# Sparse attention and a two-layer MLP in one kernel: local q and k as rows of nine tokens, and a new order for the first two batches

## The chip, the cores and the metric

One core of one Trainium2 chip runs the whole program. The time is device microseconds of one execution; the median of several runs is compared. TensorE (PE) does matmuls and transposes, VectorE (DVE) and ScalarE (ACT) elementwise work and everything that reads PSUM, GpSimd (POOL) elementwise work between SBUF tiles and the loads that cast, SyncE (SP) plain loads, stores and transposing DMAs.

## What is computed

```python
scores = q @ k.T / sqrt(64)            # 8 batches, 8 heads, 576 tokens, 64 elements
# heads 0..3 (local):   token i sees j with 0 <= i - j < 32
# heads 4..7 (strided): token i sees j <= i with j % 32 == i % 32
attn = softmax(where(mask, scores, -1e9))
x = (attn @ v) as 4608 rows of 512     # row = batch and token
h = x @ w_in                           # 512 x 2048
g = max(h, 0) + alpha * min(h, 0)      # alpha has 2048 entries
out = g @ w_out                        # 2048 x 512, float32
```

The kernel works in float16 with float32 sums.

## The kernel before

**Pairs and pieces.** Each batch has four pairs of heads: 0 and 1 local, 2 and 3 strided; pair number g = 4 * batch + pair. The work on a pair is cut into pieces:

- `Sc(g, i)` or `score_both(g)`: scores of half a pair or of all of it, the mask, and the exponential on ACT (L397 to L421 for batch 0, where the mask is added by a matmul of the constants; L455 to L487 later, where it is multiplied in on DVE or POOL).
- `Pv(g, i)`: attention times v with a column of ones (L508), the reciprocal (L515) and the scaling (L517) on DVE.
- `X(g)`: PE transposes the result (L531) and ACT or DVE copies it into `xT`, the ring of transposed rows for layer 1.
- `T(u, nm)`: PE transposes of the local q or k of a batch (L295), copied out by ACT and DVE (L235, L237).
- `F(nm, pr)`: the strided q or k of batch 0, loaded as float32 on 72 partitions (L149, eight tokens of a head to a partition) and transposed by PE as they are (L162). `G(nm, pr)`: the same for batch 1 from float16 (L174). From batch 2 on a transposing DMA does it (`transpose_d`, L184).

**Local q and k.** A load (L112 on POOL or SP, L879 for batch 0 on SP) brings eight tokens to a partition, 64 partitions to a head, so 512 tokens of 576. The last 64 tokens, the tail, come by loads of their own (`load_tail`, L209, two issues on POOL for a batch). POOL casts to float16 (`cast_l`, L239), `T` transposes eight blocks, and two more transposes (L325) and two copies serve the tails.

**v.** `load_v` fetches strided v (L219, then copied into `vs` beside the ones) and local v in overlapping blocks of 128 rows (L227); `over_v` copies the overlap of 32 rows for batches 0 and 1.

**Layers.** Rows are treated in chunks of 512. Layer 1 (`lin1_piece(n, m)`, L684) makes 16 pieces of a chunk, each four matmuls of 128x512 into one PSUM bank; ACT takes the negative part (L692) and DVE makes `gT` from it (L695). Layer 2 follows: `U` and `W` for chunk 0 (L970, L985), `lin2_piece` for chunk 1 (L723), and a form with sums and fewer products from chunk 2 on (L809).

**PSUM.** Eight banks: the pool `ps` has three (transposes, Pv), `ph` has three (layer banks, some scores, the dummy matmuls' `wps`), and `sp` takes two. A pool's tiles are given out in turn.

**Order.** Every engine runs its instructions in the order in which the program writes them (`keep`). The start is a list written by hand: nine dummy matmuls `warm(9)` (L851), then

```python
F("q", 0), F("k", 0), F("q", 1), Sc(2, 0), F("k", 1), Sc(2, 1), vs(0), w(1), Sc(3, 0), w(1), Pv(2, 0),
Sc(3, 1), Pv(2, 1), T(0, "q"), w(1), Pv(2, 2), w(1), T(0, "k"), X(2), alpha, Pv(3, 0), Sc(0, 0), w(1),
Pv(3, 1), Sc(0, 1), Pv(3, 2), w(1), Sc(1, 0), w(1), X(3), Sc(1, 1), Pv(0, 0), w(1), Pv(0, 1), L(0),
Pv(1, 0), L(1), X(0), Pv(1, 1), L(2), X(1)
```

`w(n)` are n dummies, `vs(0)` copies strided v on DVE, and `L(m)` begins piece m of layer 1 with its first two matmuls. Layer 1 of chunk 0 follows, then a second list that weaves `U` and `W` with the attention of batch 1, and from chunk 1 on a loop that takes attention pieces between the matmuls.

**Queues.** SP issues, in this order: first q load, constants 0:128 (the identity, from which DVE makes the float32 `id32`, L893), second q load, the other constants (L868), local q and k of batch 0, `alpha`. ACT issues the two first k loads. POOL issues strided v, tails, local v, w_in part 0, cast of q, w_in 1, cast of k, w_in 2 and 3; it then clears the padding rows of `qsd`, `ksd` and `x16s`, does `over_v(0)`, and issues batch 1's loads and w_out. Batch 2's loads are issued inside the second list's stretch.

Of the kernel before, what the change touches and what calls it, by code (L numbers as in the profile page):

```python
# [9 lines left out]
F32 = mybir.dt.float32  # L10
# [22 lines left out]
def kernel(  # L33
# [23 lines left out]
    tpool = ctx.enter_context(tc.tile_pool(name="tl", bufs=4))  # L57
# [40 lines left out]
    def load_qk(b, strided, nm):  # L98

        h0 = 4 if strided else 0
        src = q if nm == "q" else k
        if strided and b:
            t16 = hpool.tile([128, 2, 512], F16, tag=f"{nm}s", bufs=2, name=f"{nm}s")
            cast16[(b, True, nm)] = t16
        else:
            t16 = hpool.tile([128, 2, 512], F32, tag=f"{nm}l", bufs=2, name=f"{nm}l")
            loaded[(b, strided, nm)] = t16
        base = src[b, h0 : h0 + 1, 0:1, :]  # L110
        eng = nc.sync if (b > 2 and not strided) or (b == 0 and strided) else nc.gpsimd
        keep(eng.dma_start(t16, bass.AP(  # L112
            tensor=base.tensor, offset=base.offset,
            ap=[[8 * D, 64], [2 * S * D, 2], [S * D, 2], [1, 8 * D]])))
# [3 lines left out]
    def load_rows(b, nm):  # L118

        src = q if nm == "q" else k  # L120
        t16 = hpool.tile([128, 2048], F16, tag=f"{nm}l", bufs=2, name=f"{nm}r")
# [23 lines left out]
    def first_load(nm, pr, eng):  # L145

        src = q if nm == "q" else k
        t32 = gsum[2 * pr + (nm == "k")].rearrange("p a c -> p (a c)").bitcast(F32)[0:72]
        keep(eng.dma_start(  # L149
            t32.rearrange("p (h e) -> p h e", h=2),  # L150
            src[0, 4 + 2 * pr : 6 + 2 * pr, :, :].rearrange("h (p t) d -> p h (t d)", t=8)))
        loaded[(nm, pr)] = t32

    def turn_first(nm, pr):
# [3 lines left out]
        for h in range(2):  # L158
            pool, tag = (phpool, "hps") if h else (pspool, "ps")
            tp = pool.tile([128, 512], F32, tag=tag, name="tf")  # L160
# [25 lines left out]
    def cast_s(b, nm, eng):  # L186
        t16 = hpool.tile([128, 2, 512], F16, tag=f"{nm}s", bufs=2, name=f"{nm}s")
        if eng[0] == eng[1]:
            cast_copy(eng[0], t16, loaded[(b, True, nm)])
        else:  # L190
            for f in range(2):
                cast_copy(eng[f], t16[:, f : f + 1, :], loaded[(b, True, nm)][:, f : f + 1, :])
        cast16[(b, True, nm)] = t16

    def cast_l(b, nm, eng="pool"):
        t16 = hpool.tile([128, 8, 2, 64], F16, tag=f"{nm}l16", bufs=2, name=f"{nm}l16")
        cast_copy(eng, t16, loaded[(b, False, nm)].rearrange("p f (t d) -> p t f d", t=8))
        cast16[(b, False, nm)] = t16

    def load_tail(b, strided):  # L200

        t16 = tpool.tile([128, 512], F16, tag="tl", name="tl16")
        for i, src in enumerate((q, k)):
            if strided:
                keep(nc.gpsimd.dma_start(
                    t16[32 * i : 32 * i + 32, :].rearrange("x (h c) -> x h c", h=4),
                    src[b, 4:8, 512:576, :].rearrange("h (x c) d -> x h (c d)", c=2)))
            else:
                keep(nc.gpsimd.dma_start(  # L209
                    t16[64 * i : 64 * i + 64, 0:256].rearrange("p (h d) -> p h d", h=4),  # L210
                    src[b, 0:4, 512:576, :].rearrange("h p d -> p h d")))
        cast16[(b, strided, "tail")] = t16

    def load_v(b, strided):


        if strided:
            st = spool.tile([128, 2048], F16, tag="v", bufs=2, name="stv")
            keep(nc.gpsimd.dma_start(  # L219
                st[0:72, :].rearrange("p (h e) -> p h e", h=4),  # L220
                v[b, 4:8, :, :].rearrange("h (p t) d -> p h (t d)", t=8)))
            loaded[b] = st
        else:
# [3 lines left out]
            keep(nc.gpsimd.dma_start(  # L227
                v16[r0:128, :, 0:64],
                bass.AP(tensor=base.tensor, offset=base.offset - (32 - r0) * D,
                        ap=[[D, 128 - r0], [96 * D, 24], [1, D]])))  # L230
# [18 lines left out]
    def over_v(b, eng):  # L249

        v16 = vls[b % 2]
        cast_copy(eng, v16[0:32, 1:24, :], v16[96:128, 0:23, :])
# [28 lines left out]
    def transpose_piece(u, nm):  # L281
# [5 lines left out]
        b, strided = u // 2, u % 2 == 1  # L287
        early = b < NEARLY
        src = cast16[(b, strided, nm)]
        dst = qTs[u % 2][:, :, 0:576] if nm == "q" else kTs[u % 2][:, :, 32:608]  # L290
        tp = pspool.tile([128, 8, 64, 2], F16, tag="ps", name="tp")
        for j in range(8):
            blk = (src[:, j % 2, 128 * (j // 2) : 128 * (j // 2) + 128] if strided
                   else src[:, j].rearrange("p f d -> p (f d)"))
            keep(nc.tensor.transpose(tp[:, j].rearrange("r p e -> r (p e)"), blk, ident))  # L295
        if strided:
            main = tp.rearrange("r j p e -> r e j p")
            o = dst.rearrange("r e (j p) -> r e j p", j=8)[:, :, :, 0:64]
        else:
            main = tp.rearrange("r t p e -> r e p t")  # L300
            o = dst[:, :, 0:512].rearrange("r e (p t) -> r e p t", t=8)
        if early:
            for e in range(2):
# [3 lines left out]
                if nm == "k" and e == 1:  # L307
                    tails(b, u, strided)
# [3 lines left out]
        if nm == "k":  # L312
            tails(b, u, strided)

    def tails(b, u, strided):
# [258 lines left out]
    def X(g):  # L574
        return lambda: x_piece(pairs[g])
# [503 lines left out]
```

## Time and profile before

| | |
|---|---|
| median of 3 runs | 311.73 us (311.38 to 311.92) |
| the profiled execution | 311.1 us, span 309.2 us |
| mean granted clock of TensorE | 0.983 |
| PE busy | 295.7 us, 96% of the span |
| DVE, POOL, ACT busy | 217.0, 185.4, 174.7 us |

The profile is one execution. A line of a group names its source line, engine, operation, what it writes and reads, count, busy time, mean duration and the idle time before it with what ended most of it. A line of the timeline begins with the start in microseconds and the duration; in brackets stands the engine's idle time before it and what ended that. A busy PE is not PE at its peak: at half the granted clock the same matmuls stay busy for twice as long.

### The profile page before, as it was taken

The page shows a single profiled execution, that of the slowest core. Times are in us where ns is not written, and L with a number is a line of the kernel's source. Part 1 is how long each engine was busy: PE and PEld are TensorE (multiplying, and loading weights), DVE is VectorE, ACT ScalarE, POOL GpSimd, SP SyncE. Part 2 cuts the span into 40 slices and gives each one's busy share as a digit, 9 for nine tenths or more (in the row PEclk, how much of TensorE's full clock was granted, in tenths as well). Part 3 has the DMA queues.
Part 4 walks back from the last instruction along what each step waited for, and adds up shares of the span by engine and source line. Part 5 has one row for each costly group of instructions (what it writes and reads, how often), then busy time and mean ns, then how long its engine had stood idle before and what let it go on. Part 6 is the DMA issues. An engine that isn't in the chain of part 4 may idle for free.

```text
span 309.2 us, 6819 instructions
## 1 busy us (share of the span) xinstructions
PE 295.7 (96%) x2676; PEld 183.9 (59%) x2676; DVE 217.0 (70%) x406; ACT 174.7 (57%) x328; POOL 185.4 (60%) x175
## 2 busy tenths in 40 slices
PE   6798999799999999999999999999999999999995
PEld 2464445444455447854785478447845874685484
DVE  2356878647877589668966896689579948935861
ACT  2355672549645775577547755775476446525630
POOL 6398327633977999879897989394835403101300
PEclk9579999999999999999999999999999999999999
DMA  7999995999879597999999999997920040012003
GB/s 176 241 191 184 202 226 149 168 150 278 218 76 184 123 126 91 110 212 131 157 125 201 102 160 143 219 117 87 208 55 5 19 147 10 2 55 83 0 2 137
DMA packets 99584, 40.72 MB, mean 132 GB/s; under 512 B 78160, under 2 KB 95904, under 8 KB 99552
## 3 DMA queue, kind: packets, MB, share of 16 engines
q0 software_dynamic: 53696, 17.84, 60.4%
q1 hardware_dynamic: 45544, 21.86, 34.4%
q10 hardware_dynamic: 312, 0.59, 0.7%
q8 instruction: 21, 0.34, 0.5%
q14 instruction: 11, 0.09, 0.1%
HBM read 38.11 MB, written 9.44 MB: 154 GB/s over the span
## 4 chain that ended last, share of the span: by engine, by line
PE 76%; DVE 10%; ACT 6%; issue 3%; DMA 3%; POOL 1%; SPq 0%; ACTq 0%; DVEq 0%
PE hps L684 31%; PE ops L809 24%; PE ops L723 5%; DVE gT L695 4%; PE pv L508 4%; PE ops L970 3%; ACT neg L692 3%; DMA gsum<-in_q_dram 3%; DVE x L517 2%; PE sp L455 2%; DVE gsum L753 1%; PE xp L531 1%; PE sph L455 1%; PE tp L295 1%; ACT et L484 1%
## 5 line engine op out<-in xcount | busy, mean ns | idle before, releaser
L684 PE MATMUL hps<-xT,win 128*128 128x512 f16 x576 | 131.9, 379 | 1.1 <-DVE gT L695 0.6
L695 DVE SCALAR_TENSOR_TENSOR gT<-neg,oma,hps 128x512 f16<-128x512 f32 x144 | 105.8, 744 | 37.8 <-ACT neg L692 28.9
L692 ACT ACTIVATE neg<-hps 128x512 f32<-128x512 f32 x144 | 85.9, 597 | 37.5 <-PE hps L684 35.3
L684 PEld LDWEIGHTS <-win 128*128 128x128 f16 x576 | 53.8, 98 | 60.7 <-issue 1.9
L480 POOL TENSOR_TENSOR et<-et,consts 128x576 f16<-128x576 f16 (+1 forms) x24 | 34.7, 1445 | 37.0 <-ACT et L478 36.9
L753 POOL TENSOR_TENSOR gsum<-gT 128x1024 f16<-128x1024 f16 x14 | 29.7, 2122 | 42.2 <-DVE gT L695 37.2
L809 PEld LDWEIGHTS <-gsum 128*128 128x128 f16 x448 | 40.9, 98 | 7.1 <-DVE gsum L753 1.8
L809 PE MATMUL ops<-wsum,gsum 128*128 128x256 f16 x328 | 41.5, 273 | 0.2
L809 PEld LDWEIGHTS <-gT 128*128 128x128 f16 x336 | 31.5, 98 | 5.4 <-issue 0.3
L517 DVE TENSOR_TENSOR x<-pv,rc 96x384 f16<-96x384 f32 (+2 forms) x62 | 33.0, 532 | 2.1
L508 PEld LDWEIGHTS <-et 72*128 72x128 f16 (+1 forms) x448 | 24.3, 99 | 13.8 <-issue 2.2
L487 POOL TENSOR_TENSOR et<-et,consts 128x576 f16<-128x576 f16 (+1 forms) x24 | 31.4, 1309 | 0.0
L809 PE MATMUL ops<-wout,gT 128*128 128x256 f16 x224 | 27.9, 273 | 0.1
L478 ACT ACTIVATE et<-sp 128x576 f16<-128x576 f32 (+1 forms) x24 | 15.5, 644 | 17.2 <-PE sp L455 17.2
L515 DVE RECIPROCAL rc<-pv 72x6 f32<-72x6 f32 (+2 forms) x80 | 14.7, 184 | 13.3 <-PE pv L508 13.1
L764 DVE TENSOR_TENSOR osb<-ops,par 128x512 f32<-128x512 f32 (+1 forms) x14 | 9.4, 673 | 16.1 <-PE ops L809 8.2
L484 ACT ACTIVATE et<-sph 128x288 f16<-128x288 f32 (+1 forms) x48 | 18.8, 409 | 0.0
L762 ACT COPY osb<-ops 128x512 f32<-128x512 f32 x14 | 8.2, 585 | 16.8 <-PE ops L809 16.7
L508 PE MATMUL pv<-vs,et 72*128 72x65 f16 x256 | 16.1, 196 | 0.4 <-ACT xT L536 0.3
L723 PE MATMUL ops<-wout,gT 128*128 128x512 f16 x64 | 16.4, 379 | 0.0
L826 ACT COPY par<-ops 128x512 f32<-128x512 f32 x13 | 7.6, 585 | 13.5 <-PE ops L809 13.5
L455 PEld LDWEIGHTS <-kT 64*128 64x128 f16 x392 | 8.4, 95 | 10.5 <-issue 8.0
(109 smaller groups left out, 347.0 us busy)
## 6 DMA issues: line engine op xcount, KB each, us to landing
out_dram<-osb SPq DMA_DIRECT2D x35, 256.0 KB, 2.9
stv<-in_v_dram POOLq DMA_DIRECT2D x8, 288.0 KB, 7.9
vl<-in_v_dram POOLq DMA_DIRECT2D x6, 384.0 KB, 8.7
win<-in_moe_w_in_dram POOLq DMA_DIRECT2D x4, 512.0 KB, 10.2
wout<-in_moe_w_out_dram POOLq DMA_DIRECT2D x4, 512.0 KB, 12.3
qsd<-in_q_dram POOLq DMA_DIRECT2D x7, 288.0 KB, 6.9
ksd<-in_k_dram POOLq DMA_DIRECT2D x7, 288.0 KB, 7.3
ql<-in_q_dram SPq DMA_DIRECT2D x3, 512.0 KB, 7.7
```

What stands on the lines that cost most here:

```text
L455: keep(nc.tensor.matmul(sps[y][:, w * x : w * x + w], P.kT[hf, k0 : k0 + 128], P.qT[hf, q0 : q0 + w], start=(x == 0), stop=(x == len(grp) ...
L480: keep(nc.gpsimd.tensor_tensor(mv, mv, m, op=ALU.mult))
L484: keep(nc.scalar.activation(ev[:, n * y : n * y + n], sps[y][0:r, 0:n], AF.Exp, scale=SCALE))
L487: keep(nc.gpsimd.tensor_tensor(mv, mv, m, op=ALU.mult))
L508: keep(nc.tensor.matmul(pv[:, 65 * x : 65 * x + 65], et[0:r, c : c + 128], v16[0:r, 2 * P.pr + hh, t, :] if P.strided else v16[:, 6 * (2 * ...
L517: keep(nc.vector.tensor_tensor(P.x16[0:w, c0 : c0 + 64 * nb].rearrange("r (c e) -> r c e", e=64), pvv[:, :, 0:64], rc[0:w, 0:nb].unsqueeze ...
L684: keep(nc.tensor.matmul(hps, win16[:, kk, 128 * m : 128 * m + 128], xT[:, kk, c0 : c0 + 512], start=(kk == 2), stop=(kk == 1)))
L692: keep(nc.scalar.activation(neg, hps, AF.Relu, scale=-1.0))
L695: keep(nc.vector.scalar_tensor_tensor(gTs[n][:, m, :], neg, oma[:, m : m + 1], hps, op0=ALU.mult, op1=ALU.add))
L723: keep(nc.tensor.matmul(ops, gTs[n][:, kf, 128 * mt : 128 * mt + 128], wout16[:, kf, :], start=(kf == 0), stop=(kf == 15)))
L753: keep((nc.vector if eng == "dve" else nc.gpsimd).tensor_tensor(gsum[i][:, hs], a, b, op=op))
L809: keep(nc.tensor.matmul(o, lhs(y), rhs(y), start=(first and y == 0), stop=(y == 7), skip_group_check=True))
```

## The change

Local q and k are loaded as nine tokens to a partition, which covers all 576 tokens; the tail loads are gone. `T` transposes eight of the nine blocks as before and `tails` the ninth of q and of k, with outputs at a stride of nine. The first loads take 80 partitions for 72 (the last eight run into the next head's rows and are not used). Strided and local v of batch 0 come in two loads each. The constants are cut at 488 for 128, `alpha` goes ahead of the local loads, the rest of the constants goes last. The dummies are 17 and then 12 for 9 and then 8. The padding rows are cleared by DVE. The lists of batches 0 and 1 have a new order; `over_v` is cut into a POOL half and a DVE half for batch 0 and goes to DVE for batch 1. In chunk 0 the layer-1 pieces 3 to 5, 9 to 11 and 15 take a bank of `ps`, four pieces are begun ahead for three, and three of batch 1's `G` stand between its last pieces. Batch 2's v casts and its DMA transposes go ahead of the loop, as do a strided and a local v load of batch 3 within it.

```diff
-        t16 = hpool.tile([128, 2, 512], F32, tag=f"{nm}l", ...)
+        t32 = hpool.tile([128, 2, 576], F32, tag=f"{nm}l", bufs=2, name=f"{nm}l")
...
-        eng = nc.sync if (b > 2 and not strided) or (b == 0 and strided) else nc.gpsimd
+        eng = nc.gpsimd if b in (1, 2) else nc.sync
...
-            ap=[[8 * D, 64], [2 * S * D, 2], [S * D, 2], [1, 8 * D]])))
+            ap=[[9 * D, 64], [2 * S * D, 2], [S * D, 2], [1, 9 * D]])))
...
+            tensor=base.tensor, offset=base.offset, ap=[[8 * D, 80], [S * D, 2], [1, 8 * D]])))
...
-            pool, tag = (phpool, "hps") if h else (pspool, "ps")
-            tp = pool.tile([128, 512], F32, tag=tag, name="tf")
+            tp = pspool.tile([128, 512], F32, tag="ps", name="tf")
...
+        o = dst.rearrange("r e (p t) -> r e p t", t=9)[:, :, :, 0:8]
...
+    def tails(b, u):
+        tt = pspool.tile([128, 2, 64, 2], F16, tag="ps", name="tt")
+        for i, nm in enumerate("qk"):
+            keep(nc.tensor.transpose(
+                tt[:, i].rearrange("r p e -> r (p e)"),
+                cast16[(b, False, nm)][:, 8].rearrange("p f d -> p (f d)"), ident))
...
-            hps = phpool.tile([128, 512], F32, tag="hps", name="hps")
+            pool, tag = (pspool, "ps") if n == 0 and m // 3 % 2 else (phpool, "hps")
+            hps = pool.tile([128, 512], F32, tag=tag, name="hps")
...
-    keep(nc.sync.dma_start(consts[:, 0:128], consts_dram[:, 0:128]))
+    keep(nc.sync.dma_start(consts[:, 0:488], consts_dram[:, 0:488]))
     first_load("k", 1, nc.scalar)
     first_load("q", 1, nc.sync)
-    keep(nc.sync.dma_start(consts[:, 128:848], consts_dram[:, 128:848]))
...
-    load_l(0, "q")
-    load_l(0, "k")
     keep(nc.sync.dma_start(alpha_r, moe_alpha.rearrange("(kf p) -> kf p", p=128)))
+    load_qk(0, "q")
+    load_qk(0, "k")
+    keep(nc.sync.dma_start(consts[:, 488:848], consts_dram[:, 488:848]))
...
+    for nm in "qk":
+        keep(nc.vector.memset(qks[nm][64:80], 0.0))
+    keep(nc.vector.memset(x16s[64:80], 0.0))
...
     load_v(0, True)
-    load_tail(0, False)
     load_v(0, False)
-    load_w(0, False)
-    cast_l(0, "q")
-    load_w(1, False)
-    cast_l(0, "k")
-    load_w(2, False)
-    load_w(3, False)
+    for c in range(4):
+        load_w(c, False)
...
-    warm(9)
+    warm(17)
     for fn in [
+        F("q", 0), w(1), F("k", 0), w(2), F("k", 1), Sc(2, 0), w(1), Sc(2, 1), alpha, w(1), F("q", 1), w(2),
+        vs(0, 0), vs(0, 1), w(1), Pv(2, 0), Cl(0, "q"), Sc(3, 0), Pv(2, 2), Cl(0, "k"), Pv(2, 1), Sc(3, 1),
+        Pv(3, 0), T(0, "q"), w(1), Pv(3, 2), w(1), X(2), T(0, "k"), w(1), Pv(3, 1), w(1), ov(0, "pool", 0, 12),
+        Sc(0, 0), Sc(0, 1), X(3), Pv(0, 0), ov(0, "dve", 12, 24), Sc(1, 0), Pv(0, 1), Sc(1, 1), Pv(1, 0), L(0),
+        Pv(1, 1), L(3), L(2), X(0, "act"), X(1), L(1)]:
         fn()
+    load_d(1)
+    load_v(1, True)
+    load_w(0, True)
+    load_w(1, True)
+    load_qk(1, "q")
+    load_qk(1, "k")
+    load_w(2, True)
+    load_v(1, False)
+    load_w(3, True)
+    mid = {13: ("q", 0), 14: ("k", 0), 15: ("q", 1)}
     for m in range(16):
         lin1_piece(0, m)
         attn_n(0, 0)
+        if m in mid:
+            G(*mid[m])()
...
-        U(0), sc1(6), U(1), vs(1), U(2), sc1(7), U(3), U(4),
-        Pv(6, 0), U(5), Pv(6, 1), U(6), Pv(6, 2), U(7), Pv(7, 0), U(8), Pv(7, 1), X(6), U(9), Pv(7, 2), U(10),
-        T(2, "q"), U(11), X(7), T(2, "k"), sc1(4), W(0), W(1), sc1(5), W(2), Pv(4, 0), W(3), Pv(4, 1), W(4),
-        Pv(5, 0), X(4), W(5), Pv(5, 1), U(12), X(5), U(13), U(14), U(15), W(6), W(7)]:
+        U(0), Cl(1, "q"), G("k", 1), vs(1, 0), vs(1, 1), sc1(6), U(1), U(2), sc1(7), U(3), U(4), Cl(1, "k"), loads2,
+        Pv(6, 0), Pv(7, 0), Pv(6, 2), U(5), Pv(7, 1), U(6), T(2, "q"), Pv(7, 2), U(7), T(2, "k"), U(8), Pv(6, 1),
+        X(7, "dve"), W(0), W(1), sc1(4), U(9), W(2), sc1(5), W(3), ov(1, "dve", 0, 24), W(4), U(10), X(6), U(11),
+        Pv(4, 1), W(5), Pv(4, 0), U(12), Pv(5, 1), U(13), U(14), Pv(5, 0), U(15), W(6), X(5), X(4), W(7)]:
         fn()
+    for pr in range(2):
+        cast_v(2, pr, "pool")
     wide["on"] = False
-    load_unit(3, False)
+    transpose_d()
+    load_qk(3, "q")
+    load_qk(3, "k")
```

253 lines of the change are left out of this document (67 added, 186 removed).

## The prediction

> **What bounds the kernel now.** I read the page first: busy shares, slices, and the chain that ended last.
>
> ```profile
> PE 295.7 (96%) x2676; PEld 183.9 (59%) x2676; DVE 217.0 (70%) x406; ACT 174.7 (57%) x328; POOL 185.4 (60%) x175
> PEclk9579999999999999999999999999999999999999
> PE 76%; DVE 10%; ACT 6%; issue 3%; DMA 3%; POOL 1%; SPq 0%; ACTq 0%; DVEq 0%
> ```
>
> PE sets the end. The only slices with a low granted clock are the second and third, so I cut the span by stage (columns: PE, PEld, DVE, ACT, POOL busy with counts, clock, DMA share, GB/s).
>
> ```profile
> 0.00:10.00 10.00, 5.42 (x26) 2.45 (x27) 2.36 (x13) 2.08 (x3) 4.76 (x12) 0.94 0.83 197
> 10.00:20.00 10.00, 9.62 (x94) 6.74 (x94) 4.35 (x10) 4.47 (x11) 6.89 (x7) 0.55 1.49 208
> 20.00:31.00 11.00, 9.14 (x119) 5.73 (x119) 6.91 (x20) 6.18 (x13) 10.00 (x15) 1.00 1.21 190
> 44.00:66.60 22.60, 20.55 (x226) 11.02 (x223) 15.10 (x37) 9.29 (x21) 14.80 (x17) 1.00 1.18 144
> 66.60:83.70 17.10, 16.72 (x135) 8.19 (x134) 12.27 (x20) 14.03 (x27) 8.73 (x9) 1.00 1.19 259
> 101.80:133.00 31.20, 31.14 (x315) 20.81 (x314) 24.27 (x45) 20.64 (x38) 29.68 (x28) 1.00 1.03 109
> ```
>
> From 101.8 us on PE has 31.14 busy of 31.20: nothing is to be had there, and the change leaves that work alone. PE idle is 4.6 us before 10, 1.9 in 20 to 31, 2.05 in 44 to 66.6, 0.4 after. The stretch from 10 to 20 looks busy but runs at a clock of 0.55. So the change can move the first 31 us, a little of 44 to 66.6, and hardly anything later. Half-microsecond windows date the clock:
>
> ```profile
> 8.00:8.50 0.50, 0.00 (x0) 0.00 (x0) 0.46 (x1) 0.18 (x1) 0.00 (x0) 1.00 1.12 248
> 9.00:9.50 0.50, 0.00 (x0) 0.00 (x0) 0.00 (x0) 0.00 (x0) 0.00 (x0) 0.50 1.15 281
> 18.50:19.00 0.50, 0.50 (x5) 0.23 (x3) 0.22 (x1) 0.20 (x1) 0.50 (x1) 0.50 1.33 234
> 19.00:19.50 0.50, 0.50 (x9) 0.38 (x8) 0.18 (x1) 0.50 (x2) 0.50 (x2) 1.00 1.19 199
> ```
>
> It fell between 8.5 and 9.0 and came back at 19.0. The timeline of the start says why (start, us, engine, line, out<-in, count, idle before and what ended it):
>
> ```profile
> 1.19 4.02 PE L851 MATMUL wps<-wrm 128*128 128x512 f16 x9 [1.19 <-DVE wrm L887]
> 1.22 0.36 SPq L865 DMA_DIRECT2D consts<-consts  x1
> 1.41 0.90 POOL L219 DMA_DIRECT2D stv<-in_v_dram  x1 [0.25 <-issue]
> 2.06 0.37 SPq L868 DMA_DIRECT2D consts<-consts  x1
> 6.53 0.19 DVE L893 CAST id<-consts 72x72 f32<-72x72 f16 x1 [4.33 <-DMA consts<-consts]
> 6.78 1.22 PE L162 MATMUL tf<-id,gsum 72*128 72x72 f32 x16 [1.56 <-DVE id L893]
> 9.83 1.22 PE L162 MATMUL tf<-id,gsum 72*128 72x72 f32 x8 [1.83 <-DMA gsum<-in_q_dram]
> 12.04 0.65 ACT L421 ACTIVATE et<-sp 72x576 f16<-72x576 f32 x1 [1.03 <-PE sp L413]
> 13.37 1.42 DVE L237 COPY vs<-stv 72x1024 f16<-72x1024 f16 x2
> 25.47 0.19 DVE L515 RECIPROCAL rc<-pv 96x6 f32<-96x6 f32 x1 [1.42 <-PE pv L508]
> 28.72 0.46 DVE L237 COPY xT<-xp 128x576 f16<-128x576 f16 x1 [0.40 <-PE xp L531]
> 29.23 1.24 PE L684 MATMUL hps<-xT,win 128*128 128x512 f16 x5 [0.33 <-DVE xT L237]
> 31.07 11.38 PE L684 MATMUL hps<-xT,win 128*128 128x512 f16 x52 [0.60 <-DVE gT L695]
> ```
>
> Nine dummy matmuls end at 5.21, PE waits until 6.78 for the identity, runs 16 float transposes, and waits 1.83 us for the second q load, which stands ahead of the first scores in PE's order. The next eight transposes take the 1.22 us that sixteen took before: the gate has closed. It opens again only after the solid stretch up to 19.0.
>
> **The change, part by part.** Sums are made against the profiled execution, 311.1 us with a span of 309.2; the median of the runs shown is 311.73, 0.63 above it.
>
> *Dummies and order up to the first exponential.* Seventeen dummies replace nine. One takes 4.02/9 = 0.447 us at the start and 11.38/52 = 0.219 at full clock; the sixteen fast transposes show that the gate was open by 6.78. If it opens at about 5.2 as here, eight more end at 6.95; if it stays closed, 1.19 + 17 x 0.447 = 8.8. The identity now needs the larger constant transfer, 122 KB in place of 32. Its landing is bounded by the two transfers of the trace:
>
> ```profile
> consts<-consts SPq DMA_DIRECT2D x1, 180.0 KB, 8.8
> consts<-consts SPq DMA_DIRECT2D x1, 32.0 KB, 5.3
> stv<-in_v_dram POOLq DMA_DIRECT2D x1, 288.0 KB, 11.1
> kl<-in_k_dram SPq DMA_DIRECT2D x1, 512.0 KB, 11.5
> ```
>
> That is 1.22 + 5.3 = 6.5 or 1.22 + 8.8 = 10.0. I take 6.9, near the small one: both stand behind the first q load alone, while the 180 KB transfer stood behind the second q load too. Then three groups of eight transposes at 1.22/2 = 0.61 and three dummies at 0.22 give 6.95 + 2.5 = 9.45, and scores with their mask some 0.65 (0.99 at half clock, from 11.05 to 12.04): the first exponential starts at about 10.1, against 12.04. The second q load leaves this path; its transposes come after both score groups. The wait of 1.83 goes, and what is late next is v: the strided v lands at 1.41 + 11.1 = 12.5, while the first exponential would be done at 10.8. v now comes in two halves, so one of the two copies (1.42/2 = 0.71 each) lies before that landing, and DVE is free for the first reciprocal at 12.5 + 0.71 = 13.2. That covers late dummies as well: a first exponential at 12.0 costs nothing.
>
> *From there to the first full matmul of layer 1.* Counted on DVE, the engine with the longest chain:
>
> ```profile
> L517 DVE TENSOR_TENSOR x<-pv,rc 96x384 f16<-96x384 f32 (+2 forms) x62 | 33.0, 532 | 2.1
> L515 DVE RECIPROCAL rc<-pv 72x6 f32<-72x6 f32 (+2 forms) x80 | 14.7, 184 | 13.3 <-PE pv L508 13.1
> 20.60 0.69 DVE L237 COPY kT<-tp 128x512 f16<-128x512 f16 x1
> ```
>
> Ten Pv pieces at 0.532 + 0.184 = 7.2, a k copy 0.69, a tail copy some 0.2, the xT copy 0.46, half the overlap copy (moved here from POOL, 12 blocks of 65 columns, estimated at 0.6 from the 0.46 of 576 columns): 9.2, and 1.0 for the small gaps between 25 instructions. With no wait layer 1 could start at 13.2 + 10.2 = 23.4. Waits are added: DVE's idle time in 20 to 31 was 11.00 - 6.91 = 4.1, which gives 27.5 as the other end. I take 1.6, since one round trip from k's transposes through scores and exponential to the first local Pv must stay (1.42 at 25.47): 25.0, against 29.23.
>
> *Banks.* Before, layer 1 had three banks: at 31.07, after a stall of 0.60 for the first gT, 64 - 52 = 12 matmuls were done. Now four pieces are begun ahead (8 matmuls) and pieces 3 to 5, 9 to 11 and 15 use the other pool, so piece 6 is the first to wait for a gT. Twelve are done at 25.0 + 4 x 0.219 = 25.9: the gain up to here is 31.07 - 25.9 = 5.2.
>
> *Queues.* POOL no longer issues ten tail loads and no longer clears the three padding tiles; DVE does that, inside its 4.33 us of waiting for the constants. POOL's casts grow by an eighth (nine tokens for eight), under cover of loads that are in flight anyway. All four w_in loads are issued at once; on the one software queue they still stand behind v, as the first did before. Batch 1's loads are issued earlier, and the tails' small packets are gone, so the later loads stand no further back. The local q and k loads grow from 512 to 576 KB each, and the first loads from 288 to 320: 256 KB more ahead of the k cast, about 1.0 us at the 248 to 281 GB/s of the windows above. k would land by 3.24 + 11.5 + 1.0 = 15.7 and be cast by 15.7 + 1.04 x 9/8 = 16.9, earlier by what the tails' packets took; its transposes, behind q's, I place at about 16.5. That is just about covered, so a later landing is a rival below.
>
> ```profile
> 3.24 0.61 SPq L879 DMA_DIRECT2D kl<-in_k_dram  x1
> 14.81 1.04 POOL L239 CAST kl<-kl 128x1024 f16<-128x1024 f32 x1 [0.24 <-DMA kl<-in_k_dram]
> 43.92 0.81 PE L970 MATMUL ops<-wout,gT 128*128 128x512 f16 x3
> ```
>
> *Chunk 0's layer 2 with batch 1's attention (from 43.92).* Three of the four transposes of batch 1 move into the end of layer 1, and the list is reordered so that consecutive pieces wait less for a bank. Of PE's 2.05 idle I take 0.5 as saved; the ends are all of it, and a loss of 1.0 because the whole overlap copy of batch 1 (by the same estimate 1.2) now stands on DVE ahead of the local Pv pieces. *Batch 2 and 3:* v casts, DMA transposes and a v load leave the first steps of the next loop; of 0.4 idle there I take 0.2.
>
> Sum: 5.2 + 0.5 + 0.2 = 5.9 faster, 311.1 - 5.9 = 305.2 for a profiled execution and 311.73 - 5.9 = 305.8 for the median.
>
> Beside the clock rows: the Trainium skill, "TensorE: Matmul & The Clock Gate", Part 1: The HAM clock gate, says that the gate judges activity in free-running windows of about 3.4 us, and that the ramp costs under 1% of a typical kernel, so one should not fit to a count of cold matmuls. The trace agrees with windows and not with the 1% (an estimate by that page, 3.1 us here): 10 us at half clock can hide up to 5 us of work. By the page's figure the gain to layer 1 would be at most 3.1 + 1.0 for the banks, and the sum 4.8.
>
> **The rivals.** *The gate closes again* (chance 0.14). Between 12.5 and 19 PE waits for DVE again and again, and I count it busy for some 60 to 75% of that time. A stretch with 1.22 us of work in 3.4 closed it above; the 83% of 20 to 31 did not. If it closes once more, up to 3.4 us of work run at half speed before layer 1: about 2.8 lost, gain 3.1, 308.6.
>
> *Loads come late* (0.10). If the larger transfers put the local k 3 us later than 14.7, its cast (about 1.2) ends at 18.9, 2.4 after the transposes could start: layer 1 at 27.4, gain 3.5, 308.2. For it: DMA runs at a share over 1.1 from 5 us on. Against: the tails are gone.
>
> *Slower: the constants hold up everything* (0.09). If the 122 KB land like the 180 KB, at 10.0, PE idles from 6.95 to 10.2, the gate closes as before, and three groups at 1.22 with three dummies at 0.447 bring the scores to 15.2, 4.2 later than before. With the 14.9 us from first exponential to layer 1 of the forecast, stretched to 16 by the closed gate, layer 1 starts at 32.2; less 1.7 for banks and later parts the kernel is 1.3 slower, and 0.2 slower unstretched: 312.5 in the middle. It decides from a landing at about 9.3 on. The Trainium skill, "DMA: Bandwidth & Descriptors", Why a DMA increments its semaphore by 16 and not by 1, says that such a load uses the largest count of engines up to 16 that divides its rows: 12 for 72 rows, 16 for 80; by that the first loads would clear the way sooner and this rival would deserve half its chance. No view shows single engines.
>
> *It does nothing that shows* (0.02): v's landing sets the start however the order is. Against it, v was in at 12.5 and the first reciprocal came only after 13.37 + 1.42 = 14.8.
>
> **How the numbers follow.** The forecast has 0.65, with its own range from 303.2 to 307.6 (layer 1 from 23.4, with 1.0 more out of the later parts, to 26.8). Most likely 305.8. The range of 303.6 to 309.4 takes in the two partial gains and leaves out the slower case, no change and the forecast's best end, together about 0.2. Faster by over 0.2% (0.6 us, about what a measurement of this kernel can tell from no change): 0.65 + 0.14 + 0.10 = 0.89; same 0.02; slower 0.09.
>
> **What would show it.** The clock row should stay at full from the second slice on; first float transposes near 7.0 with no wait between groups; first exponential near 10; first reciprocal near 13.4, waiting for v; layer 1 in full near 25.0 and no wait for gT on PE in chunk 0; U's first matmul near 38. Wrong, if PE idles over a microsecond ahead of the first transposes, if a half clock appears after 10 us, or if layer 1 starts after 28.

## The result and the profile after

| | before | after |
|---|---|---|
| median | 311.70 us (311.38 to 312.04, 6 runs) | 306.68 us (306.46 to 307.54, 6 runs) |
| ratio | | 0.9842, 95% interval 0.9828 to 0.9856 |
| span of the profiled execution | 309.2 us | 304.5 us |
| mean granted clock | 0.983 | 1.000 |

The change gains 5.0 us where 5.9 were forecast; the time lies 0.9 above the number given and inside its range. The page of the changed kernel, in the same three lines as before:

```profile
PE 294.4 (97%) x2688; PEld 182.3 (60%) x2688; DVE 223.4 (73%) x413; ACT 176.1 (58%) x326; POOL 175.6 (58%) x163
PEclk9999999999999999999999999999999999999999
PE 79%; DVE 10%; ACT 6%; issue 2%; DMA 2%; SPq 0%; DVEq 0%; ACTq 0%
```

The clock is full in every slice. The windows (PE, PEld, DVE, ACT and POOL busy with counts, clock, DMA share, GB/s) say the same, and the last one says something new:

```profile
0.00:10.00 10.00, 8.64 (x53) 4.38 (x54) 4.92 (x17) 2.48 (x4) 7.42 (x18) 1.00 0.86 202
10.00:20.00 10.00, 8.16 (x116) 5.09 (x116) 6.90 (x19) 6.13 (x12) 6.34 (x8) 1.00 1.48 223
96.00:127.00 31.00, 29.97 (x298) 19.59 (x296) 24.31 (x44) 19.83 (x38) 28.74 (x27) 1.00 1.06 117
```

In the stretch that was solid before (31.14 busy of 31.20, chunk 2) PE is now idle for 1.03 us. The timeline of the start, with a few instructions of each step:

```profile
1.19 5.96 PE L768 MATMUL wps<-wrm 128*128 128x512 f16 x17 [1.19 <-DVE wrm L788]
7.08 0.19 DVE L797 CAST id<-consts 72x72 f32<-72x72 f16 x1 [2.10 <-DMA consts<-consts]
7.32 0.72 PE L153 MATMUL tf<-id,gsum 72*128 72x72 f32 x8 [0.17 <-DVE id L797]
10.33 0.65 ACT L337 ACTIVATE et<-sp 72x576 f16<-72x576 f32 x1 [0.44 <-PE sp L329]
12.13 0.46 DVE L209 CAST qT<-tf 128x288 f16<-128x288 f32 x1 [0.65 <-PE tf L153]
12.51 1.17 DVE L209 COPY vs<-stv 72x1024 f16<-72x1024 f16 x2
13.48 0.34 PE L424 MATMUL pv<-vs,et 72*128 72x65 f16 x6 [0.74 <-DVE vs L209]
13.87 0.19 DVE L431 RECIPROCAL rc<-pv 72x6 f32<-72x6 f32 x1 [0.19 <-PE pv L424]
19.41 0.30 PE L313 MATMUL sp<-qT,kT 64*128 64x96 f16 x6 [0.95 <-ACT kT L207]
24.96 11.04 PE L601 MATMUL hps<-xT,win 128*128 128x512 f16 x50
38.35 0.81 PE L884 MATMUL ops<-wout,gT 128*128 128x512 f16 x3
```

The dummies last until PE can start on the transposes, 0.17 us of idle apart; the second q load no longer stands in the way; fifty matmuls of layer 1 run without a wait for `gT`. The starts of the same work in the two traces:

| start, us | before | after | gain |
|---|---|---|---|
| first exponential | 12.04 | 10.33 | 1.7 |
| layer 1 in full | 29.23 | 24.96 | 4.3 |
| first matmul of U | 43.92 | 38.35 | 5.6 |
| layer 1 of chunk 1 | 66.43 | 60.32 | 6.1 |
| layer 2 of chunk 1 | 83.57 | 77.58 | 6.0 |
| layer 2 of chunk 2 | 101.61 | 95.87 | 5.7 |
| layer 1 of chunk 3 | 132.87 | 128.26 | 4.6 |
| end of the span | 309.2 | 304.5 | 4.7 |

The gain reaches 6.1 us and then loses 1.5 between 60 and 128 us. PE's waits in the changed kernel from 40 to 130 us name the place (total, times, longest):

```profile
PE sp L371 <- ACT kT L207: 1.6, 3, 0.8
PE xp L447 <- ACT kT L207: 0.7, 1, 0.7
PE tt L286 <- ACT qT L207: 0.5, 1, 0.5
```

The three waits of the scores end at 68.09, 88.05 and 119.48 us (0.56, 0.19 and 0.82) and make up the loss; the other two lie before 50 us. In the kernel before, the stretch from 66 to 133 us has no wait for `kT`. The timeline shows the longest of the three, first after, then the same place before:

```profile
117.96 0.71 DVE L209 COPY qT<-tt 128x128 f16<-128x128 f16 x1
118.71 0.72 ACT L207 COPY kT<-tt 128x128 f16<-128x128 f16 x1 [1.16 <-DVE qT L209]
119.48 0.30 PE L371 MATMUL sp<-qT,kT 64*128 64x96 f16 x6 [0.82 <-ACT kT L207]
```

```profile
123.45 0.21 DVE L237 COPY qT<-tt 128x128 f16<-128x128 f16 x1
123.70 0.27 ACT L235 COPY kT<-tt 128x128 f16<-128x128 f16 x1 [0.66 <-DVE qT L237]
124.10 0.30 PE L455 MATMUL sp<-qT,kT 64*128 64x96 f16 x6
```

The two copies of the ninth token take 0.71 and 0.72 us where those of the tails took 0.21 and 0.27, and ACT's waits for DVE's: 1.47 us in a row for 0.52.

### The profile page after: what moved, and what is told of

The parts are those of the page before. It is cut to its first block, busy times and chain, and to the rows that moved or that the text cites. A ratio compares the mean times of both kernels' runs of the same rounds, so it can differ in the third digit from the quotient of the medians.

```text
span 304.5 us, 6839 instructions
## 1 busy us (share of the span) xinstructions
PE 294.4 (97%) x2688; PEld 182.3 (60%) x2688; DVE 223.4 (73%) x413; ACT 176.1 (58%) x326; POOL 175.6 (58%) x163
## 4 chain that ended last, share of the span: by engine, by line
PE 79%; DVE 10%; ACT 6%; issue 2%; DMA 2%; SPq 0%; DVEq 0%; ACTq 0%
PE hps L601 36%; PE ops L726 24%; PE ops L640 4%; PE pv L424 4%; DVE gT L612 3%; DVE gsum L670 2%; PE sp L371 2%; PE ops L884 2%; DMA consts<-consts 2%; ACT neg L609 2%; DVE qT L209 1%; PE sph L371 1%; PE xp L447 1%; ACT kT L207 1%; PE ops L899 1%
## 5 line engine op out<-in xcount | busy, mean ns | idle before, releaser
L424 PEld LDWEIGHTS <-et 72*128 72x128 f16 (+1 forms) x448 | 23.2, 98 | 12.5 <-issue 1.8
L431 DVE RECIPROCAL rc<-pv 96x6 f32<-96x6 f32 (+2 forms) x80 | 14.6, 183 | 10.2 <-PE pv L424 10.2
L211 POOL COPY vs<-stv 72x1024 f16<-72x1024 f16 x12 | 13.4, 1118 | 6.7 <-DMA stv<-in_v_dram 6.7
L424 PE MATMUL pv<-vs,et 72*128 72x65 f16 x256 | 15.2, 193 | 0.8 <-DVE vs L209 0.7
```

Source lines behind the costliest of these rows:

```text
L424: keep(nc.tensor.matmul(pv[:, 65 * x : 65 * x + 65], et[0:r, c : c + 128], v16[0:r, 2 * P.pr + hh, t, :] if P.strided else v16[:, 6 * (2 * ...
```

## The experiments

The times are medians; the ratio is to the kernel before in the same group of runs (312.13, 311.49 and 312.04 us in the three groups), to be held against the 0.9842 of the change. In the third group the runs of before scatter up to 314.98, so that its ratios lie lower than the medians say; there medians and spans are compared.

That scatter goes with the mean granted clock of each execution: in the third group the kernel before takes 311.19 to 311.86 us at 0.983 and 0.978, 313.12 and 313.37 at 0.973, and 314.67 to 314.98 at 0.966. Executions listed at 1.000 don't fit: 311.95 and 312.04 there, and 311.23 to 315.04 for the kernel without the dummies below. No trace of one of these was kept, so whether they ran at full clock stays open. The clock is therefore read from the kept traces, where the matmuls' lengths bear it out: eight float transposes take 0.67 to 0.72 us in the change, and 1.22 in the stretch at half clock before.

### The clock alone

The kernel before with more dummies, in two versions. The first:

```diff
-    warm(9)
+    warm(16)
-        F("q", 0), F("k", 0), F("q", 1), Sc(2, 0), F("k", 1), Sc(2, 1), vs(0), w(1), Sc(3, 0), w(1), Pv(2, 0),
+        F("q", 0), F("k", 0), w(8), F("q", 1), w(1), Sc(2, 0), w(1), F("k", 1), w(1), Sc(2, 1), vs(0), w(4), Sc(3, 0), w(3), Pv(2, 0),
...
```

> The kernel before with more dummy matmuls and nothing else: sixteen at the start, nine between the first transposes, and twenty more through the stretch up to 20 us. Theory (the gain is the sum of clock, order and banks): the clock stays full, the first exponential comes near 11, the first reciprocal near 14.0 (v lands at 12.5, then two copies of 0.71), layer 1 in full near 26, and the time is 308.7, a gain of 3.0. Rival one, the clock is the whole gain: 306.7. Rival two, loads and DVE set the start and a faster PE only waits more: 311.1 to 311.7.

310.57 us, ratio 0.9956 (0.9942 to 0.997), clock 1.000: a gain of 1.4. Layer 1 in full came at 28.30. The first reciprocal came only at 15.54, behind seven dummies where the kernel before has two, so a second version went with twelve fewer (2696 matmuls in its trace for 2708).

> The kernel before with dummies again and nothing else, but ten fewer than in the first run of this kind, since there the first reciprocal came at 15.54 behind seven dummies and a score group on PE while DVE had been idle for 2.35. Theory (clock and order each need the other: a full clock alone meets the old order, in which v's copies, the scores and the dummies stand ahead of the first attention piece): first reciprocal near 14.6, layer 1 in full near 27.5, gain 2.0 to 2.5, time 309.3 to 309.8. Rival, the clock is the larger part of the gain of 5.0 and the first run only hid it under its own dummies: below 308.5.

310.54 us, ratio 0.9967 (0.9948 to 0.9986), clock 0.999. The first reciprocal moved to 14.80 and the time didn't follow. Its timeline says what was late next:

```profile
24.03 0.31 PE L508 MATMUL pv<-vl,et 128*128 128x65 f16 x5 [1.50 <-POOL vl L239]
```

PE, at full clock, stood 1.50 us for the overlap copy of local v, which in the kernel before is one piece of POOL's queue, after both casts and the clearing of three tiles. The change cuts it in two and moves it. Every gain that was expected of the clock here (2.0 to 5.0) was too high: in the old order a full clock is worth 1.0 to 1.4 us, with the time that the added dummies take on PE already taken off.

### The order without the dummies

```diff
-    warm(17)
+    warm(9)
-        F("q", 0), w(1), F("k", 0), w(2), F("k", 1), Sc(2, 0), w(1), Sc(2, 1), alpha, w(1), F("q", 1), w(2),
+        F("q", 0), F("k", 0), F("k", 1), Sc(2, 0), Sc(2, 1), alpha, F("q", 1),
...
```

> The changed kernel with nine dummies at the start for seventeen and none of the twelve later ones; the order stays. Theory: the clock falls to half again near 9 us, comes back only after the solid stretch of layer 1 begins or shortly before it, layer 1 in full comes 2 to 3 us later than 24.96, and the time is 309 to 309.7. Rival, the new order with DVE and the loads as its bound doesn't need the clock: 306.7 within 0.6.

311.22 us (310.18 to 315.04 in twelve executions), ratio 0.9979 (0.9949 to 1.0009): nearly the whole gain is gone, 4.5 us, more than expected. Half-microsecond windows, the pair where the clock falls and the pair where it comes back:

```profile
7.50:8.00 0.50, 0.50 (x9) 0.50 (x7) 0.08 (x1) 0.38 (x1) 0.50 (x4) 0.65 1.18 221
27.50:28.00 0.50, 0.50 (x2) 0.15 (x1) 0.47 (x2) 0.17 (x1) 0.33 (x1) 0.50 1.21 199
28.00:28.50 0.50, 0.50 (x8) 0.31 (x7) 0.25 (x2) 0.00 (x0) 0.43 (x1) 0.87 1.25 187
```

The clock was half from 7.65 (0.65 of a window that starts at 7.50) to 28.13, 20.5 us, twice as long as in the kernel before. There PE ran almost solid from 9.83 us until the clock came back at 19.0; the new order leaves it waits (0.97 us at 14.04, 1.23 at 22.10 for a k copy). That these waits kept the clock down fits, but no run tests it. So the clock alone brings 1.0 to 1.4, the rest of the change without the added dummies 0.5 to 0.9 (its interval reaches zero), and both together 5.0. Neither number is a share of the gain; each part needs the other. The rest holds the rows of nine tokens, the loads, the banks and both lists; what the rows of nine tokens or the new order of the loads give by themselves, no run shows.

### Late dummies

```diff
-    warm(17)
+    warm(25)
```

> The changed kernel with 25 dummies at the start, which puts everything on PE 8 x 0.219 = 1.75 us later. The prediction held that a first exponential at 12.0 costs nothing, since v lands at 12.5: then the time is 306.7 within 0.3. Theory after the trace: DVE copies v only after its copy of the second q's transposes, which PE now reaches at 13.2, so the first reciprocal moves from 13.87 to 15.6, layer 1 in full from 24.96 to 26.4 or later, and the time is 308.1 to 308.4.

308.25 us, ratio 0.9886 (0.9866 to 0.9905): 1.4 (by ratios) to 1.6 us (by medians) slower than the change. The DVE timeline:

```profile
14.28 0.46 DVE L209 CAST qT<-tf 128x288 f16<-128x288 f32 x1 [0.65 <-PE tf L153]
14.65 1.00 DVE L209 COPY vs<-stv 72x1024 f16<-72x1024 f16 x2
15.84 0.19 DVE L431 RECIPROCAL rc<-pv 72x6 f32<-72x6 f32 x1 [0.19 <-PE pv L424]
```

The v copies follow the cast of the second q's transposes, which PE reaches later; both halves of v had landed by 12.0. The first reciprocal is 1.97 later than in the change, layer 1 in full 1.82 (26.78). There was no slack behind the first exponential.

### Banks

```diff
-            pool, tag = (pspool, "ps") if n == 0 and m // 3 % 2 else (phpool, "hps")
+            pool, tag = phpool, "hps"
-        Pv(1, 1), L(3), L(2), X(0, "act"), X(1), L(1)]:
+        Pv(1, 1), L(2), X(0, "act"), X(1), L(1)]:
```

> The changed kernel with all banks of layer 1 of chunk 0 from the pool of three, as before, and three pieces begun ahead for four. The prediction's term for the banks is 1.0 us (0.60 stall plus two matmuls begun ahead, 0.44): 307.7, with a wait of PE for gT of about 0.6 near 27 us. Rival, ACT and DVE hold the same pace with three banks and the matmuls only move: 306.7 within 0.3.

308.32 us, ratio 0.989 (0.9872 to 0.9908): 1.5 to 1.6 us slower. Its timeline has the expected stall and a second one, ahead of the last matmul of U's first group:

```profile
27.76 9.66 PE L601 MATMUL hps<-xT,win 128*128 128x512 f16 x44 [0.60 <-DVE gT L612]
41.13 0.38 PE L884 MATMUL ops<-wout,gT 128*128 128x512 f16 x1 [0.75 <-DVE gT L612]
```

Of the difference of the spans (2.2 us) some 0.5 is the start of this execution, where the first transposes began at 7.85 for 7.32.

### The copies of the ninth token left out

Batches 1 to 4 don't copy the ninth tokens of q and k; their scores use older values there.

```diff
-            cast_copy(eng, o.rearrange("r e (p t) -> r e p t", t=9)[:, :, :, 8],
-                      tt[:, i].rearrange("r p e -> r e p"))
+            if b == 0:
+                cast_copy(eng, o.rearrange("r e (p t) -> r e p t", t=9)[:, :, :, 8],
+                          tt[:, i].rearrange("r p e -> r e p"))
```

> The changed kernel without the copies of the ninth token in batches 1 to 4 (eight copies of 0.72 left out, so those rows of q and k keep older values). Theory: these copies, 0.72 on DVE and then 0.72 on ACT where it was 0.22 and 0.27, hold PE at k's first scores, and cost most of the 1.4 us that the gain loses between 60 and 128 us: 305.3 to 305.8. Rival, they lie beside other work and the loss comes from banks or from loads of batches 2 and 3: 306.4 to 306.9.

304.73 us, ratio 0.9782 (0.9765 to 0.9798): 1.9 us faster than the change by medians and by ratios, more than expected. From layer 1 of chunk 1 (60.58) to that of chunk 3 (126.69) it takes 66.11 us, where the change takes 67.94 and the kernel before 66.44: without the copies the loss of 1.5 is gone, and a little more, since the old tails had copies too (0.52 a batch). From 40 to 130 us PE no longer waits for `kT`, and two other waits have come up in their place (the overlap copy of batch 1's v takes 1.37 there, see below):

```profile
PE pv L425 <- DVE vl L209: 0.7, 1, 0.7
PE pv L425 <- DVE et L392: 0.3, 1, 0.3
```

### A tile for each of the two copies

```diff
-        tt = pspool.tile([128, 2, 64, 2], F16, tag="ps", name="tt")
+        tts = [pspool.tile([128, 64, 2], F16, tag="ps", name="tt") for _ in range(2)]
```

> The changed kernel with a PSUM tile of its own for q's and for k's ninth token, so that ACT's copy of k doesn't wait for DVE's copy of q: in the changed kernel each reads one half of one tile, and the second is made to wait for the first. Theory: that wait, up to 0.72 in each of five batches, is a part of what PE waits for; 305.7 to 306.2. Rival, the second tile out of a pool of three makes PE wait for a bank by as much: 306.5 or more.

305.95 us, ratio 0.9826 (0.981 to 0.9841), span 303.8: 0.7 us less than the change by median and by span, though the intervals of the ratios overlap. The copies of a batch now run side by side, and the pool of three shows in a wait:

```profile
116.74 0.73 ACT L207 COPY kT<-tt 128x128 f16<-128x128 f16 x1 [0.22 <-PE tt L286]
116.94 0.71 DVE L209 COPY qT<-tt 128x128 f16<-128x128 f16 x1
```

```profile
PE tt L286 <- DVE x16s L433: 1.0, 1, 1.0
```

The time is in the range of the theory, but not for its reason alone. From layer 1 of chunk 1 (59.63) to that of chunk 3 (127.56) this kernel takes 67.93 us, no less than the change (67.94): a pair of copies is done in 0.91 us for 1.47, and PE waits 0.99 for the bank instead (at 116.47) and 0.41 for a copy of q (at 85.97). There the rival holds. The 0.7 us lies ahead of chunk 1, and 0.2 of it is the start of this execution, where the first transposes began at 7.12 for 7.32. The Trainium skill, PSUM — Partial Sum Buffer, section PSUM bank collisions raise a hardware error, says that the compiler puts a dependency between any two instructions of different engines on one bank, two readers included; the trace agrees: ACT waited for DVE as long as they read halves of one tile, and not with two.

### Six tokens and three

```diff
-        for t in range(8):
+        for t in range(6):
...
-                cast16[(b, False, nm)][:, 8].rearrange("p f d -> p (f d)"), ident))
+                    cast16[(b, False, nm)][:, 6 + t].rearrange("p f d -> p (f d)"), ident))
...
-            cast_copy(eng, o.rearrange("r e (p t) -> r e p t", t=9)[:, :, :, 8],
+            cast_copy(eng, o.rearrange("r e (p t) -> r e p t", t=9)[:, :, :, 6:9],
```

> The changed kernel with blocks cut 6 and 3 for 8 and 1: the two main copies of a batch take six tokens of nine, and the two tail copies three, 384 elements in runs of three. Theory one, the copy of 128 elements is slow because each run is a single element of two bytes and longer runs cost less: a tail copy takes 0.45 to 0.55, the main copies 0.2 less, k's tail is there 0.5 sooner in each batch, and the time is 305.7 to 306.2. Theory two, the price goes by the run, 5 ns each: a tail copy takes 0.75 to 0.85, and the time is 306.4 to 306.9. Theory three, it goes by the element at this stride: 1.5 us or more, and 308 or more.

306.56 us, ratio 0.9853 (0.9833 to 0.9872): no different from the change. The groups by shape (busy, mean ns of one), of this kernel and then of the change:

```profile
L207 ACT COPY kT<-tt 128x384 f16<-128x384 f16 x5 | 3.6, 725 | 4.1 <-DVE qT L209 3.4 <-DVE rc L432 0.7
L209 DVE COPY qT<-tt 128x384 f16<-128x384 f16 x5 | 3.6, 716 | 1.4 <-PE tt L287 1.4
L207 ACT COPY kT<-tp 128x768 f16<-128x768 f16 x3 | 2.5, 831 | 1.4 <-PE tp L266 1.4
```

```profile
L207 ACT COPY kT<-tt 128x128 f16<-128x128 f16 x5 | 3.6, 724 | 2.9 <-DVE qT L209 2.6 <-DVE rc L431 0.3
L209 DVE COPY qT<-tt 128x128 f16<-128x128 f16 x5 | 3.6, 717 | 1.2 <-PE tt L286 1.2
L207 ACT COPY kT<-tp 128x1024 f16<-128x1024 f16 x3 | 3.0, 1015 | 1.3 <-PE tp L266 1.3
```

Three times the elements take the same 0.72, on both engines. All of these copies write 128 runs on each partition, whose starts lie 18 bytes apart; with runs of one or three elements they take 0.72, of six 0.83, of eight 1.02 (six and eight on ACT alone). So the price goes by the run up to some five elements (0.72/128 = 5.6 ns, the fixed part included) and by the element beyond (256 more elements cost 0.18): theory two. That the copies read PSUM at a stride as well is not the price: in the kernel before, ACT's copies of 1024 elements read at a stride too, write 512 in a row and take 1.01, some 1 ns an element; by that, 128 elements would add 0.13 (an estimate). The Trainium skill, SBUF — State Buffer, section Door 1: The DMA port swizzle, says that SBUF has lines of 16 bytes and that each access that crosses to a new line pays a penalty, without a price for writes. The runs don't show such a line as what costs here: 128 runs of one element lie on 128 lines and 128 runs of three reach into about 144 (64 runs over 1152 bytes, twice), and both take 0.72.

### Each operand's ninth token behind its own eight

```diff
-        if nm == "k":
-            tails(b, u)
+        tail(b, u, nm, "dve")
...
+        tt = pspool.tile([128, 64, 2], F16, tag="ps", name="tt")
```

> The changed kernel with each operand's ninth token transposed and copied right behind its own eight: a PSUM tile for each, q's copy long before k's, and from batch 2 on both on DVE beside ACT's main copies. Theory: the price of a copy is fixed at 0.72 by its 128 separate runs, so only its place can be changed; off the serial chain on ACT k is ready about 0.7 sooner than with own tiles alone, and the time is 305.1 to 305.7 (304.7 with the copies left out). Rival, DVE's queue, 75% busy there, holds the copies up and PE waits for DVE as it did for ACT: 306.0 or more.

305.87 us, span 303.6: 0.8 and 0.9 less than the change, between the two ranges. PE's waits are now small and spread (0.4 at most). The sum is about what two tiles alone gave, but it lies where the copies do: from layer 1 of chunk 1 (60.41) to that of chunk 3 (127.33) this kernel takes 66.92 us, 1.0 less than the change, and ahead of that nothing is gained.

### Strided v's copies taken apart

```diff
-        ..., Sc(2, 1), alpha, w(1), F("q", 1), w(2), vs(0, 0), vs(0, 1), w(1), Pv(2, 0), Cl(0, "q"),
+        ..., Sc(2, 1), vs(0, 0), alpha, F("q", 1), w(1), Pv(2, 0), vs(0, 1), w(1), Cl(0, "q"),
```

> The changed kernel with strided v's two copies on DVE taken apart: the first one directly behind the first scores' transposes, the first attention piece (which reads only that half) ahead of the second, and one dummy fewer in front. Theory: the first reciprocal in the changed kernel (13.87) waits for the order on DVE and PE, not for v, whose first half landed at 9.94; it now comes near 12.2, layer 1 in full near 23.5, and the time is 305.2 to 305.8. Rival one, k's landing (14.0, cast to 15.2) and v's halves bind next: layer 1 near 24.5, 306.2 or more. Rival two, layer 1 comes earlier but batch 1's weights and loads, which don't, give it back before 60 us: 306.2 to 306.7 with layer 1 at 23.5.

305.96 us, span 304.6, between the ranges of the theory and of rival two. The edit takes out two dummies in all. The start does what it should:

```profile
12.39 0.19 DVE L431 RECIPROCAL rc<-pv 72x6 f32<-72x6 f32 x1
23.76 3.60 PE L601 MATMUL hps<-xT,win 128*128 128x512 f16 x15
```

The first reciprocal is 1.48 earlier and layer 1 in full 1.20, but layer 1 of chunk 1 starts at 60.47 where the change has 60.32: all is given back before 60 us. The larger part goes at one wait that the change doesn't have, from 36 to 60 us:

```profile
PE pv L424 <- DVE vl L209: 0.7, 1, 0.7
```

The copy that PE waits for is the overlap of batch 1's local v, and beside it ran POOL's cast of batch 2's k:

```profile
53.41 1.46 POOL L211 CAST kl<-kl 128x1152 f16<-128x1152 f32 x1 [0.69 <-DMA kl<-in_k_dram]
53.89 1.37 DVE L209 COPY vl<-vl 32x1495 f16<-32x1495 f16 x1
```

In the change the same copy runs after that cast (which runs from 52.72 to 53.87) and takes 0.54:

```profile
54.58 0.54 DVE L209 COPY vl<-vl 32x1495 f16<-32x1495 f16 x1
```

A stage that starts earlier met a neighbour that starts later (53.41 for 52.72), because the cast waits for its load: rival two in kind, with a load of batch 2. It is this meeting, too, that stretched the copy to 1.37 where the ninth tokens were left out; both times the copy starts second and ends 0.39 after the cast. Where the copy starts first, it isn't held up and the cast is. This is the kernel with first loads of 72 partitions, below:

```profile
55.44 0.54 DVE L209 COPY vl<-vl 32x1495 f16<-32x1495 f16 x1
55.58 1.41 POOL L211 CAST kl<-kl 128x1152 f16<-128x1152 f32 x1 [1.37 <-DMA kl<-in_k_dram]
```

In the change the same cast takes 1.15. The median is 0.7 below the change's, the span the same; whether something is left of this edit by itself stays open.

### Both

> The two edits, v's copies taken apart and a tail copy for each operand behind its own, together in the changed kernel. If the two gains lie at different places (before 25 us, and from 44 us on) they add: 303.8 to 304.6. If what comes earlier waits for batch 1's loads, only the second remains: 305.1 to 305.7.

304.98 us (304.38 to 305.62), span 302.9, clock 0.998, ratio 0.9745 (0.9703 to 0.9787): 1.7 us less than the change by median and 1.6 by span, a version that beats both kernels. The two edits add up (0.8 or 0.9 for the tail copies, 0.7 to 0.9 more for v's), short of the 2.1 to 2.9 expected of them. Here the overlap copy of batch 1 takes 0.54 again, with no cast beside it, and layer 1 of chunk 1 starts at 59.71, 0.61 before the change's and 0.70 before that of the kernel with the tail copies alone (60.41). From there to layer 1 of chunk 3 it takes 66.92 us, as with the tail copies alone. So the two gains lie at different places, which was the condition for adding up.

### First loads of 72 partitions

```diff
-        t32 = ....bitcast(F32)[0:80]
+        t32 = ....bitcast(F32)[0:72]
-            ..., ap=[[8 * D, 80], [S * D, 2], [1, 8 * D]])))
+            ..., ap=[[8 * D, 72], [S * D, 2], [1, 8 * D]])))
```

> The changed kernel with first loads of 72 partitions for 80, 288 KB each for 320. By the rule of the Trainium skill (DMA: Bandwidth & Descriptors, Why a DMA increments its semaphore by 16 and not by 1) such a load is spread over 12 engines for 16, so the last of the four, the second q load, lands later than 9.43, by up to a third of its own time. Rival, the loads share what the whole chip path gives and a tenth less data lands sooner: 9.0 to 9.4. Either way PE reaches those transposes only at 11.43, and the time stays at 306.2 to 307.2.

307.38 us in the one run, span 305.4. The first five microseconds of this kernel, of the change and of the kernel before (72 partitions too):

```profile
0.00:5.00 5.00, 3.81 (x9) 1.34 (x10) 3.56 (x13) 1.28 (x1) 4.21 (x12) 1.00 0.47 139
```

```profile
0.00:5.00 5.00, 3.81 (x9) 1.34 (x10) 3.56 (x13) 1.28 (x1) 4.21 (x12) 1.00 0.60 153
```

```profile
0.00:5.00 5.00, 3.81 (x9) 1.20 (x9) 1.25 (x10) 1.28 (x1) 4.22 (x12) 1.00 0.51 138
```

A mean DMA share of 0.47 for 0.60 is close to 12 engines for 16; the rate falls by a tenth, as the loads themselves do (288 KB for 320); local k landed at 14.57 for 14.01. The kernels with 80 partitions lie between 0.59 and 0.63, those with 72 between 0.47 and 0.51. That agrees with the rule; the landing of the second q load itself doesn't show in this trace. What wasn't expected is the clock:

```profile
15.50:16.00 0.50, 0.44 (x8) 0.47 (x9) 0.47 (x2) 0.00 (x0) 0.27 (x1) 0.93 1.75 198
19.00:19.50 0.50, 0.50 (x8) 0.36 (x6) 0.50 (x2) 0.30 (x1) 0.50 (x2) 0.65 1.25 209
```

It was half from 15.93 to 19.35, with all of the dummies in place: 3.42 us, which makes the mean clock of 0.994. The 72 partitions need not be the reason: of the six executions of the change itself one has 0.994 too, and took 307.54 us. Against that one this run isn't slower, and the one time says nothing of what the loads cost.

## Why the prediction was right, and where not

**The clock, right; its worth by itself, too high.** The clock stayed full, and the closed gate was the rival to fear: without the dummies the change loses 4.5 us. But the prediction held that the 10 us at half clock of the old order can hide up to 5 us, and a full clock in that order brought 1.0 to 1.4. The Trainium skill, TensorE: Matmul & The Clock Gate, Part 1: The HAM clock gate, gives windows of about 3.4 us; the half clock lasted 3.42 in the last experiment, about 10.2 in the kernel before and 20.5 without dummies, one, three and six such windows. The traces agree with the windows. On the cost of a ramp, under 1% of a typical kernel by that section, the runs are divided: 1.0 to 1.4 of 312 us in the old order is under 0.5%, 4.5 of 306.7 in the new one, with six windows, is 1.5%. The sum of 4.8 by that section's figure came nearer to 5.0 than the forecast's 5.9 did, but by luck: it allowed 4.1 for the gain up to layer 1 with the banks, which was 5.57 at U, and the copies of the ninth token took the difference back.

**The first transposes, right.** The larger constants were in by 7.05 (forecast 6.9), the dummies ended at 7.15, the first exponential came at 10.33 (10.1).

**The first reciprocal, right in number, wrong in cause.** It came at 13.87 (13.2 to 13.4). The prediction had v's landing set it and called a later exponential free. v's halves were in at 9.94 and 11.97; what set it was DVE's order, where the v copies stand behind the cast of the second q's transposes. The late dummies cost 1.4 to 1.6 us where the prediction has them cost nothing; and the copies taken apart brought the reciprocal to 12.39 with v landing no earlier.

**DVE's chain, right; the start of layer 1, right by luck.** From the first reciprocal to the end of the last copy into `xT` (25.16 + 0.46 = 25.62) it took 11.75 us, 8.70 of them busy; the prediction had 11.8, 9.2 of them busy. Since the reciprocal was late, that copy was late too, 25.62 for 25.0. PE could start at 24.96 all the same, because the first two matmuls there don't need it. So 24.96 for 25.0 is not the same work: six matmuls of layer 1 were done by then and not eight, twelve by about 26.3 (24.96 + 6 x 0.22) and not 25.9, and the gain up to there is 4.8 for the 5.2 counted.

**Banks, right, but too low.** They are worth 1.5 to 1.6 us for the 1.0 counted (0.60 and two matmuls): the second stall, 0.75 ahead of U, wasn't seen.

**Queues, right.** Local k landed at 14.0, well ahead of its transposes at 17.13; the rival of late loads had no part.

**Batch 1's stretch, right in sum.** The gain grew from 5.57 at U to 6.11 at chunk 1's layer 1, 0.54 for the 0.5 taken, though two waits for the copies of ninth tokens lie in it.

**The tail copies, wrong.** "A tail copy some 0.2" was carried over from a copy of the same 128 elements that wrote runs of 64. The new one writes 128 runs of one and takes 0.72, the second behind the first. The pair of them stands five times in the kernel, and the sum counted one copy once and at the old price. From chunk 1 on the prediction expected 0.2 more; the trace lost 1.5 there, and leaving out the copies of four batches gives 1.9 back, 0.5 a batch, where the pair grew by 0.95 (1.47 for 0.52). In the profiled executions the three terms of the sum, 5.2, 0.5 and 0.2, measured 5.6 (at U), 0.5 and a loss of 1.5; at the end of the span 4.7 is left. The step that failed is that "the change leaves that work alone" from 101.8 us on: the new rows are transposed and copied there too.

## What to carry to other kernels

A copy's price must be read for its access pattern and not for its element count: the same 128 elements cost 0.22 us in runs of 64 and 0.72 in runs of one, and an operand that is relaid once is copied again in every batch. Dummy matmuls and a better order should be tried together: here either alone brought about a quarter of the gain or less. A full clock ran into the next wait, and in the new order the clock stayed down without dummies. Before calling a step covered by a landing, look at what stands ahead of its reader in that engine's queue.

## What the runs showed of the hardware

- Strided writes of 2-byte elements: 0.72 us for 128 runs of one or three elements on ACT and on DVE; on ACT 0.83 for six and 1.02 for eight.
- The half clock came in pieces of about 3.4 us (3.42, 10.2, 20.5), and one such piece appeared with all dummies in place (first loads of 72 partitions; by the mean clock of 0.994 also in one of the six executions of the change), so the dummies have little margin; why it did isn't shown.
- With first loads of 80 partitions for 72 the mean DMA share of the first 5 us is 0.60 for 0.47, and the rate 153 GB/s for 139, the loads being larger by as much.
- The overlap copy of 1495 columns on 32 partitions took 0.54 us on DVE, where POOL had taken 1.53, and 1.37 when a cast on POOL had started before it (twice); when it started 0.14 before the cast, it took 0.54 and the cast 1.41 for 1.15 (once). The prediction's estimate was 1.2.
